# Reordering the prologue of a Fourier-mixing and gated-FFN kernel: loads, fillers and the stages of the first two batches

## The chip, the cores and the metric

The kernel runs on one core of one Trainium2 chip. The metric is the device time of one execution in microseconds. Before the change three runs took 904.98, 905.38 and 907.63 us; their median, 905.38, is the time before.

## What is computed

The reference mixes a sequence in the frequency domain and then applies a gated feed-forward network to every row:

```
X = rfft(x, axis=1);  Y = X * (filt_r + 1j*filt_i);  y = irfft(Y, n=3008, axis=1)   # x: 8 x 3008 x 256
gate = max(y @ w_gate, 0);  val = y @ w_val                                          # 256 x 1536 each
out = (gate * val) @ w_out                                                           # 1536 x 256
```

The output has 24064 rows of 256, in 32-bit floats.

## The kernel before

The 3008 points are split as 94 x 32, so that a transform is three stages of small matrix products, with two passes through DRAM ("bounces") between them.

Stage A (items_a, L269, matmul L276) is a 94-point transform: for each batch 16 items, each one 128x512 product of WA with a part of x (tiles XF, two of them, each 16 of the 32 columns wide), a copy by ScalarE into asb (L279), and after every fourth item a 384 KB write to Abuf (L281). Stage B reads Abuf back as at (load_at, L349, four loads of 384 KB), does 32-point transforms (fwd, L363), multiplies with the filters (product, L379: tt and uu; in batch 0 seven of the uu go by a ScalarE copy xs, L376, to GpSimd, L377), transforms back (inv, L393), copies (L400) and writes Dbuf (L402). There are six such excursions (i = 0 to 5) in a batch; inv of excursion i-2 stands behind fwd of excursion i. Stage C reads Dbuf back as dC (load_d, L425, four quarters of two loads), and item_c (L448) makes the transposed rows yT of one block of 512 rows. The network follows: gv (L464) makes psV and psG of one of 12 slices of the 1536 features, ScalarE copies psV (L467), VectorE multiplies (L469), and o_part (L483) makes the output of the block before.

From batch 2 on stage A is done in another way (load_chunk, fold_chunk, tiled_a; x goes through XP tiles that take the memory of the prologue). Batches 0 and 1 use items_a.

The order is written out by hand: each engine runs its instructions in the order of the program. Every DMA of SyncE goes into one queue, and a DMA that waits for a semaphore holds up those behind it; GpSimd's DMAs (filters, weights, XP) stand in order with its arithmetic. There are eight semaphores for each kind of DMA, taken in turn, so the ninth waits for the first to land.

The prologue of before: memsets of XF (L512 to L518; x has 94 rows, so some partitions stay zero), x of batch 0 by SyncE (load_x, L177) in pieces of half a tile, the DFT tables (F2, tabs, WF), and by GpSimd the filters behind a hold (hold_gpsimd, L258: a tiny copy that waits for a tile). TensorE runs 11 warm matmuls (products of a tile junk that nobody reads, L508), then the 16 items of stage A, each followed by one 128x256 filler matmul up to item 12, and by make_back_t (L193, sixteen 64x64 matmuls that transpose F2 into I2t) from item 13 on. Then come three make_back_u (L203) with six warm matmuls each, and 18 more. Meanwhile VectorE copies I2t (L198), doubles the filters in place (place_filter, L238) and places tables (L210 to L242). After the at loads SyncE issues a tiny DMA named gate (L555), which reads at and so waits until all of at is there, and only then x of batch 1. GpSimd, behind a hold on at, issues the first halves of Wv and Wg (load_vg, L246).

Then stage B of batch 0 (first_b, L405): after excursions 0 and 1 a function amid runs three fillers, after excursions 2, 3, 4 and 5 it runs 1, 2, 2 and 2 items of stage A of batch 1. Behind it stand the first quarter of dC, the tiny load "last" (L571, which waits for the last write of Dbuf), the second halves of Wv and Wg, Wo (L252), the 9 items of stage A that are left, and item_c of block 0.

The main loop (L627) runs 47 blocks of 12 steps. Work of the next batches is hung on steps (at_step): quarters 1 to 3 of dC of batch 0 on steps 0, 9 and 14, all four at loads of batch 1 on step 3, fwd of excursions 0 to 5 of batch 1 on steps 16, 23, 26, 29, 35 and 40 (end = 51), those of later batches at end - 40, -35, -28, -23, -16 and -11.

```
for i, l in enumerate((-35, -28, -25, -22, -16, -11, -4) if b == 1 else
                      (-40, -35, -28, -23, -16, -11, -4)):
```

Of the kernel before, what the change touches and what calls it, by code (L numbers as in the profile page):

```python
# [13 lines left out]
BF16 = mybir.dt.bfloat16  # L14
# [17 lines left out]
NG = 24  # L32
# [3 lines left out]
def _ap(t, offset_elems, ap_list):  # L36
    return dataclasses.replace(
        t, offset=t.offset + offset_elems, ap=[list(p) for p in ap_list]
    )
# [81 lines left out]
def kernel(  # L121
# [10 lines left out]
    nc = tc.nc  # L132
    B, S_, D = x.shape
    DFF = moe_w_gate.shape[1]
# [13 lines left out]
    dram = ctx.enter_context(tc.tile_pool(name="dram", bufs=1, space=bass.MemoryType.DRAM))  # L148
# [3 lines left out]
    pro = prologue.enter_context(tc.tile_pool(name="pro", bufs=1))  # L152

    Abuf = [dram.tile([NROW * N2, D], BF16, name=f"Abuf{b}") for b in range(B)]
    gate = dram.tile([32, 8], BF16, name="gate")
    Dbuf = [dram.tile([NROW * N2, D], BF16, name=f"Dbuf{b}") for b in range(B)]

    XF = [pro.tile([128, NX2 * D], FP32, name=f"XF{c}") for c in range(N2 // NX2)]
# [13 lines left out]
    def load_x(b, eng, cols):  # L172
        w = NX2 * D
        for c, c0, c1 in cols:
            for m in range(3):
                rows = min(32, B * N1 - (b * N1 + 32 * m))
                eng.dma_start(XF[c][m:m + 4 * rows - 3:4, c0:c1],  # L177
                              _ap(x, (b * N1 + 32 * m) * N2 * D + c * w + c0,
                                  [[N2 * D, rows], [1, c1 - c0]]))
# [7 lines left out]
    def make_back_t(q):  # L187

        psI = [ps.tile([128, 4, 64], FP32, tag=fft_tag(), name="psI") for _ in range(2)]
        for e in range(2):  # L190
            for a in range(2):
                for j in range(4):
                    nc.tensor.matmul(psI[e][64 * a:64 * a + 64, j],  # L193
                                     F2[64 * e:64 * e + 64, 12 * a + 4 * q + j, :],
                                     perm[64 * e:64 * e + 64], start=True, stop=True,
                                     tile_position=(64 * e, 64 * a))
        for e in range(2):
            nc.vector.tensor_copy(I2t[:, 8 * q + e:8 * q + 8:2, :], psI[e])  # L198
# [45 lines left out]
    def load_vg(c0, c1):  # L244
        for (w_hbm, w_sb) in ((moe_w_val, WvT), (moe_w_gate, WgT)):
            nc.gpsimd.dma_start(w_sb[:, :, c0:c1],  # L246
                                _ap(w_hbm, c0, [[DFF, 128], [128 * DFF, 2], [1, c1 - c0]]))

    def load_o():
        for c in range(2):  # L250
            nh = NFT // 2
            nc.gpsimd.dma_start(WoT[:, c * nh:(c + 1) * nh],  # L252
                                _ap(moe_w_out, c * nh * 128 * D, [[D, 128], [128 * D, nh], [1, D]]))
# [9 lines left out]
    def fft_tag(side=False):  # L263
        if side and turn.get("side"):
            return turn["side"]
        turn["i"] += 1
        return turn["tags"][turn["i"] % len(turn["tags"])]
# [76 lines left out]
    ats = {}  # L344

    def load_at(b, c):
        if c == 0:
            ats[b] = sb.tile([128, NG, D], BF16, tag="at", bufs=1, name="at")
        nc.sync.dma_start(ats[b][c:c + 125:4],  # L349
                          _ap(Abuf[b], c * NROW * NC2 * D, [[D, 32], [4 * NC2 * D, NG], [1, D]]))  # L350
# [31 lines left out]
    def inv(b, i, tags=None, cuts=CUTS):  # L382

        if i in cuts:
            dsbs[b] = i, sb.tile([128, 2, 4, D], BF16, tag="dsb", bufs=3, name="dsb")
        i0, dsb = dsbs[b]
        psD = [ps.tile([128, 2, D], FP32, tag=tags[a] if tags else fft_tag(), name="psD")
               for a in range(2)]
        for m in range(2):
            for k in range(2):  # L390
                for a in range(2):
                    for e in range(2):
                        nc.tensor.matmul(psD[a][64 * e:64 * e + 64, m],  # L393
                                         (I2t, I2u)[k][64 * a:64 * a + 64, 4 * i + 2 * m + e, :],
                                         tus[b, i, e, k][64 * a:64 * a + 64, m],
                                         start=(k == 0), stop=(k == 1),
                                         tile_position=(64 * a, 64 * e))
        o = 2 * (i - i0)
        for a in range(2):
            nc.scalar.copy(dsb[:, a, o:o + 2, :], psD[a])  # L400
        if i + 1 in cuts:
            nc.sync.dma_start(_ap(Dbuf[b], 2 * i0 * D, [[NG * D, 128], [NG // 2 * D, 2], [1, (o + 2) * D]]),  # L402
                              dsb[:, :, :o + 2, :])

    def first_b(amid):  # L405

        cuts = (0, 2, 4, 5, 6)
        for i in range(6):
            fwd(0, i)
            if i > 1:  # L410
                inv(0, i - 2, cuts=cuts)
            for e in range(2):
                product(0, i, e, 0)
                product(0, i, e, 1, pool=(i, e) in POOL_U)
            amid(i)
        inv(0, 4, cuts=cuts)
        inv(0, 5, cuts=cuts)

    dCs = {}
# [82 lines left out]
    junk = pro.tile([128, 512], BF16, tag="junk", bufs=1)  # L502

    def warm(n, cols=512):

        psJ = ps.tile([128, 512], FP32, tag=fft_tag(True), name="psJ")
        for i in range(n):
            nc.tensor.matmul(psJ[:, :cols], junk[:, 0:128], junk[:, :cols], start=True, stop=True)  # L508

    nc.sync.dma_start(WA, nc.inline_tensor(wa_h, name="dft_wa").ap())  # L510
    q = NX2 * D // 4
    nc.vector.memset(XF[0][:, 0:q], 0.0)  # L512
    nc.gpsimd.memset(XF[0][:, q:2 * q], 0.0)
    nc.vector.memset(junk, 1.0)
    nc.vector.memset(XF[0][:, 2 * q:3 * q], 0.0)
    nc.gpsimd.memset(XF[0][:, 3 * q:], 0.0)
    nc.vector.memset(XF[1][:, 0:2 * q], 0.0)
    nc.gpsimd.memset(XF[1][:, 2 * q:], 0.0)  # L518
    load_x(0, nc.sync, ((0, 0, 2 * q), (0, 2 * q, 4 * q), (1, 0, 2 * q)))
    nc.sync.dma_start(F2, nc.inline_tensor(f2_h, name="dft_f2").ap())  # L520
    nc.sync.dma_start(tabs, nc.inline_tensor(tab_h, name="dft_tab").ap())
    load_x(0, nc.sync, ((1, 2 * q, 4 * q),))
# [7 lines left out]
    warm(11)  # L530
    for i, f in enumerate(items_a(0)):
        f()
        if i >= 13:
            make_back_t(i - 13)
        else:
            warm(1, 256)
        if i == 11:
            load_at(0, 0)
    for c in range(1, 4):
        load_at(0, c)  # L540
    for half in range(2):
        for a in range(2):
            place_filter(0, a, half, nc.vector.tensor_copy)
    for i in range(3):
        make_back_u(i)
        warm(6)
    warm(18)
    place_own()
    for half in range(2):
        for a in range(2):  # L550
# [1 line left out]
    place_nyq()  # L552
    hold_gpsimd(ats[0][0:32, NG - 1, 0:8])
    load_vg(0, DFF // 2)
    nc.sync.dma_start(gate, ats[0][0:32, NG - 1, 0:8])  # L555
    load_x(1, nc.sync, ((0, 0, 2 * q), (0, 2 * q, 4 * q), (1, 0, 4 * q)))

    early = items_a(1)
# [1 line left out]
    def amid(i):  # L560
        if i < 2:
            warm(3, 256)
        else:
            for _ in range(2 if i > 2 else 1):
                next(early)()

    turn["tags"], turn["side"] = ("fft", "psv", "psg"), "pso"
    first_b(amid)
# [1 line left out]
    load_d(0, 0, 1)  # L570
    nc.gpsimd.dma_start(pro.tile([1, D], BF16, tag="last", bufs=1, name="last"),  # L571
                        _ap(Dbuf[0], (N2 * NROW - 1) * D, [[D, 1], [1, D]]))
    load_vg(DFF // 2, DFF)
    load_o()
    for f in early:
        f()
    for h in range(2):
# [13 lines left out]
    def at_step(s, f):  # L591
        side.setdefault(s, []).append(f)
# [5 lines left out]
    for b in range(1, B):  # L598
        end = (b * S // W - 1) * NFT + C_AT[0] - 5
        if b == 1:  # L600
            for c in range(4):
                at_step(3, lambda c=c: load_at(1, c))
        else:
            for j, e in enumerate((-74, -69, -64, -57)):
                l = end - 113 + NFT * j

                def next_x(b=b, j=j, l=l):
                    hold_gpsimd(yTs[l // NFT + 1][:, 0, 0:8])
                    load_chunk(b, j)
                    if j:  # L610
                        fold_chunk(b, j - 1)
                    if j == 3:
                        fold_chunk(b, j)
                at_step(l, next_x)
                at_step(end + e, lambda b=b, j=j: tiled_a(b, j))
            at_step(end + e + 4, lambda b=b: load_at_tiled(b))
        for i, l in enumerate((-35, -28, -25, -22, -16, -11, -4) if b == 1 else
                              (-40, -35, -28, -23, -16, -11, -4)):
            if i < 6:
                at_step(end + l, lambda b=b, i=i: fwd(b, i))  # L620
                for h in range(4):
                    at_step(end + l + h, lambda b=b, i=i, h=h: product(b, i, h // 2, h % 2))
            if i > 0:
                at_step(end + l, lambda b=b, i=i: inv(b, i - 1, ("psv", "psg")))
        at_step(end - 2, lambda b=b: load_d(b))
# [42 lines left out]
```

## Time and profile before

| what | us |
|---|---|
| median of three runs | 905.38 |
| the profiled execution | 907.27 |
| its span (first to last instruction) | 905.5 |
| TensorE busy in the span | 875.3 |
| stage A of batch 0, first item starts | 7.46 |
| last item of it ends (its copy starts) | 23.80 |
| stage B of batch 0, first fwd | 33.44 |
| stage B ends and the items of stage A of batch 1 that are left begin | 54.48 |
| stage C, first psY | 62.83 |
| first psV of block 0 | 63.90 |
| psY of block 1 at dC's second quarter | 75.82 |
| first fwd of batch 1 | 87.63 |

Busy us of TensorE in stretches of 10 us from 0: 6.85, 10.00, then two that the prediction shows, 7.89, 10.00, 9.11, 6.41, 8.15, 9.95; from 100 to 120 us 17.67 of 20, from 120 on 19.84 of every 20. The DMA engines' mean busy share in the first ten of these stretches is 0.64, 1.11, 1.14, 0.71, 1.00, 0.45, 1.07, 1.25, 0.97 and 0.37.

How to read it: TensorE is busy for 97% of the span, so a time is made of its work plus its gaps. A line of the waits gives who waited, for whom, the total, how often, and the longest. In the chain of waits a line is a start, a length and what ran then. A DMA's landing is the last of the sixteen increments of its semaphore.

### The profile page before, as it was taken

How to read it: one execution, taken by the hardware profiler on the slowest of the kernel's cores; microseconds unless marked ns; L12 is line 12 of the kernel's file. 1: busy time of each engine (PE TensorE's matmuls, PEld its weight loads, DVE VectorE, ACT ScalarE, POOL GpSimd, SP SyncE). 2: the span in 40 equal slices, each digit the busy share in tenths (PEclk: the TensorE clock that was granted, in tenths of full speed). 3: DMA queues.
4: the chain of work that ended last, by engine and by line, in shares of the span. 5: the costliest groups of instructions: out<-in, count | busy, mean ns of one | idle time of the engine just before them, and what ended most of it. 6: DMA issues, size and time to landing. Idle time of an engine off the chain costs nothing.

```text
span 905.5 us, 19111 instructions
## 1 busy us (share of the span) xinstructions
PE 875.3 (97%) x7096; PEld 512.1 (57%) x7217; DVE 566.6 (63%) x872; ACT 498.6 (55%) x891; POOL 359.0 (40%) x351
## 2 busy tenths in 40 slices
PE   8797899999999999999999999999999999999997
PEld 3343565556555665566655566556655556666665
DVE  2635776567665776657766677657766577655553
ACT  4474556555555555555655565655565555555552
POOL 4342667117680386614763166811768000000000
PEclk9899999999999999999999999999999999999999
DMA  9979337623475344663364533754346512331111
GB/s 254 245 219 220 101 95 177 141 80 109 122 175 118 90 126 122 141 134 112 96 161 128 119 98 101 182 116 100 108 136 158 116 31 82 78 75 36 37 32 51
DMA packets 113662, 109.17 MB, mean 121 GB/s; under 512 B 20290, under 2 KB 98370, under 8 KB 112834
## 3 DMA queue, kind: packets, MB, share of 16 engines
q1 hardware_dynamic: 91078, 81.72, 35.3%
q0 software_dynamic: 22176, 26.01, 11.7%
q8 instruction: 57, 0.93, 0.5%
q10 hardware_dynamic: 316, 0.22, 0.1%
q14 instruction: 35, 0.29, 0.1%
HBM read 61.93 MB, written 49.81 MB: 123 GB/s over the span
## 4 chain that ended last, share of the span: by engine, by line
PE 86%; DVE 4%; DMA 4%; ACT 3%; issue 1%; SPq 1%; POOL 0%; DVEq 0%; POOLq 0%
PE psG L464 25%; PE psO L483 25%; PE psV L464 24%; DVE prod L469 4%; PE psA L276 3%; PE psF L322 3%; ACT vsb L467 3%; PE psD L393 2%; PE psX L363 2%; PE psY L448 1%; DMA XF<-in_x_dram 1%; DMA dC<-Dbuf 1%; DMA Abuf<-asb 1%; DMA out_dram<-osb 0%; DMA at<-Abuf 0%
## 5 line engine op out<-in xcount | busy, mean ns | idle before, releaser
L469 DVE SCALAR_TENSOR_TENSOR prod<-psG,vsb 128x512 bf16<-128x512 f32 x564 | 389.0, 690 | 271.3 <-ACT vsb L467 265.8
L467 ACT CAST vsb<-psV 128x512 bf16<-128x512 f32 x564 | 333.0, 590 | 266.8 <-PE psV L464 211.7
L483 PE MATMUL psO<-WoT,prod 128*128 128x256 bf16 x2256 | 336.6, 273 | 1.5
L464 PE MATMUL psG<-yT,WgT 128*128 128x512 bf16 x1099 | 329.1, 379 | 7.4 <-DMA WgT<-in_moe_w_gate_dram 2.5
L464 PE MATMUL psV<-yT,WvT 128*128 128x512 bf16 x1037 | 316.9, 380 | 0.7 <-ACT yT L453 0.4
L483 PEld LDWEIGHTS <-prod 128*128 128x128 bf16 x2256 | 220.7, 98 | 143.4
L464 PEld LDWEIGHTS <-WgT 128*128 128x128 bf16 x1128 | 109.9, 98 | 136.9 <-DMA WgT<-in_moe_w_gate_dram 3.0
L464 PEld LDWEIGHTS <-WvT 128*128 128x128 bf16 x1128 | 98.1, 98 | 41.8 <-issue 30.4
L258 POOL CAST scr<-yT 128x8 f32<-128x8 bf16 x24 | 4.6, 191 | 265.8 <-ACT yT L453 265.8
L379 DVE TENSOR_TENSOR tt<-psX,Ftr 128x512 bf16<-128x512 f32 x96 | 65.0, 682 | 12.9 <-PE psX L363 12.9
L400 ACT CAST dsb<-psD 128x512 bf16<-128x512 f32 x96 | 51.5, 589 | 28.5 <-PE psD L393 28.4
L308 POOL TENSOR_TENSOR fold<-XP 128x1024 f32<-128x1024 f32 x24 | 56.5, 2356 | 25.1 <-PE psF L322 24.9
L489 ACT COPY osb<-psO 128x512 f32<-128x512 f32 x92 | 54.5, 593 | 20.6 <-PE psO L483 20.3
L379 DVE TENSOR_TENSOR uu<-psX,Fti 128x512 bf16<-128x512 f32 x89 | 60.6, 681 | 0.0
L309 POOL TENSOR_TENSOR XP<-XP 128x1024 f32<-128x1024 f32 x24 | 56.4, 2350 | 1.9
L295 POOL DMA_DIRECT2D XP<-in_x_dram x96 | 56.4, 592 | 0.9 <-issue 0.5
L453 ACT CAST yT<-psY 128x512 bf16<-128x512 f32 x47 | 27.6, 586 | 26.2 <-PE psY L448 26.2
L329 DVE CAST asb<-psF 128x512 bf16<-128x512 f32 x48 | 30.9, 686 | 17.3 <-PE psF L322 12.9
L329 ACT CAST asb<-psF 128x512 bf16<-128x512 f32 x48 | 25.8, 589 | 27.3 <-PE psF L322 27.3
L448 PE MATMUL psY<-M,dC 96*128 96x94 bf16 (+18 forms) x604 | 37.7, 198 | 1.1 <-DMA dC<-Dbuf 1.1
L455 DVE CAST yT<-psY 128x512 bf16<-128x512 f32 x47 | 32.0, 681 | 9.8 <-PE psY L448 9.8
L448 PEld LDWEIGHTS <-dC 96*128 96x128 bf16 x604 | 34.5, 97 | 4.6 <-DMA dC<-Dbuf 1.2
(66 smaller groups left out, 481.6 us busy)
## 6 DMA issues: line engine op xcount, KB each, us to landing
at<-Abuf SPq DMA_DIRECT2D x32, 384.0 KB
dC<-Dbuf SPq DMA_DIRECT2D x64, 192.0 KB
XP<-in_x_dram POOLq DMA_DIRECT2D x48, 256.0 KB, 5.9
Dbuf<-dsb SPq DMA_DIRECT2D x23, 512.0 KB
XP<-in_x_dram POOLq DMA_DIRECT2D x96, 96.0 KB, 2.7
Abuf<-asb SPq DMA_DIRECT2D x96, 96.0 KB
out_dram<-osb SPq DMA_DIRECT2D x70, 94.0 KB
XF<-in_x_dram SPq DMA_DIRECT2D x18, 256.0 KB
```

What stands on the lines that cost most here:

```text
L295: nc.gpsimd.dma_start(xp[r:r + 24, 0:4:2, :], _ap(x, (b * N1 * N2 + o) * D, [[N2 * D, 24], [47 * N2 * D, 2], [1, 512]]))
L308: tt(t, xp[:, 0:2], xp[:, 2:4], op=ALU.add)
L309: tt(xp[:, 2:4], xp[:, 0:2], xp[:, 2:4], op=ALU.subtract)
L329: copy(asf[:, :, q, :], banks[q])
L379: nc.vector.tensor_tensor(p, psX, filt, op=ALU.mult)
L400: nc.scalar.copy(dsb[:, a, o:o + 2, :], psD[a])
L448: nc.tensor.matmul(psY[:, o:o + w], dCs[b, n2 // 8][:, n2 % 8, h * 128:(h + 1) * 128], M1[:, n1:n1 + w], start=True, stop=True)
L464: nc.tensor.matmul(pt[:, :W], w[:, h, ft * 128:(ft + 1) * 128], yt[:, h, :], start=(h == 0), stop=(h == 1))
L467: nc.scalar.copy(vsb, psV[:, :W])
L469: nc.vector.scalar_tensor_tensor(prod, in0=psG[:, :W], scalar=0.0, in1=vsb, op0=ALU.max, op1=ALU.mult)
L483: nc.tensor.matmul(psO[:, t % 2], prods[ft][:, t * 128:(t + 1) * 128], WoT[:, ft, :], start=(ft == 0), stop=(ft == NFT - 1))
L489: copy(osb[:, t0 % 2:t % 2 + 1], psO[:, t0 % 2:t % 2 + 1])
```

## The change

- The first half of XF's first tile is loaded in two quarters, and the memsets ahead of it are smaller; GpSimd and VectorE each clear half of the first quarter, and junk is cleared right after.
- In stage A of batch 0 the fillers are gone. The make_back_t stand behind it, with six warm matmuls each, and the 18 warm matmuls ahead of stage B become 6.
- The gate DMA is gone: x of batch 1 is issued right behind the at loads.
- amid runs 1, 2, 2, 2 items after excursions 2 to 5, and one more between the last two inv; 8 are left behind stage B.
- The second halves of Wv and Wg are issued amid excursion 4, no longer behind "last".
- Two of the at loads of batch 1 are issued behind dC's first quarter, the two others on steps 0 and 1.
- Batch 1's stage B runs at the steps of later batches: fwd at 11, 16, 23, 28, 35 and 40.

```diff
-    gate = dram.tile([32, 8], BF16, name="gate")
...
         inv(0, 4, cuts=cuts)
+        amid(6)
         inv(0, 5, cuts=cuts)
...
-    nc.vector.memset(XF[0][:, 0:q], 0.0)
+    nc.gpsimd.memset(XF[0][:, 0:q // 2], 0.0)
+    nc.vector.memset(XF[0][:, q // 2:q], 0.0)
+    nc.vector.memset(junk, 1.0)
     nc.gpsimd.memset(XF[0][:, q:2 * q], 0.0)
-    nc.vector.memset(junk, 1.0)
...
-    load_x(0, nc.sync, ((0, 0, 2 * q), (0, 2 * q, 4 * q), (1, 0, 2 * q)))
+    load_x(0, nc.sync, ((0, 0, q), (0, q, 2 * q), (0, 2 * q, 4 * q), (1, 0, 2 * q)))
...
         f()
-        if i >= 13:
-            make_back_t(i - 13)
-        else:
-            warm(1, 256)
         if i == 11:
             load_at(0, 0)
     for c in range(1, 4):
         load_at(0, c)
+    for i in range(3):
+        make_back_t(i)
+        warm(6)
...
-    warm(18)
+    warm(6)
...
-    nc.sync.dma_start(gate, ats[0][0:32, NG - 1, 0:8])
     load_x(1, nc.sync, ((0, 0, 2 * q), (0, 2 * q, 4 * q), (1, 0, 4 * q)))
...
-            for _ in range(2 if i > 2 else 1):
+            for _ in range((1, 2, 2, 2, 1)[i - 2]):
                 next(early)()
+        if i == 4:
+            load_vg(DFF // 2, DFF)
...
-    load_vg(DFF // 2, DFF)
     load_o()
+    for c in range(2):
+        load_at(1, c)
...
-            for c in range(4):
-                at_step(3, lambda c=c: load_at(1, c))
+            for c in range(2, 4):
+                at_step(c - 2, lambda c=c: load_at(1, c))
...
-        for i, l in enumerate((-35, -28, -25, -22, -16, -11, -4) if b == 1 else
-                              (-40, -35, -28, -23, -16, -11, -4)):
+        for i, l in enumerate((-40, -35, -28, -23, -16, -11, -4)):
```

## Prediction

> **What bounds the kernel now.** I read the page first, then the waits of TensorE over the whole run and after 130 us, then the busy times by stage, the chain of waits and the timeline of VectorE, and last the landing events of every DMA (the last of the sixteen increments of its semaphore).
>
> ```profile
> PE 875.3 (97%) x7096; PEld 512.1 (57%) x7217; DVE 566.6 (63%) x872; ACT 498.6 (55%) x891; POOL 359.0 (40%) x351
> ```
>
> TensorE is the bound: only 905.5 - 875.3 = 30.2 us are not its own. The waits of TensorE say where they lie:
>
> ```profile
> PE psA L276 <- DMA XF<-in_x_dram: 4.4, 2, 3.8
> PE psG L464 <- DMA WgT<-in_moe_w_gate_dram: 2.5, 1, 2.5
> PE psJ L508 <- DVE junk L514: 2.5, 1, 2.5
> PE psX L363 <- DVE uu L379: 2.2, 2, 1.1
> PE psX L363 <- issue: 1.8, 1, 1.8
> PE psD L393 <- POOL uu L377: 1.4, 2, 0.8
> PE psY L448 <- DMA dC<-Dbuf: 1.1, 2, 0.7
> ```
>
> The same view from 130 us on has no entry at all: every stall is in the prologue and batch 1's stage B, which is what the change touches. The busy times by stage (columns: stretch, length, then busy us of PE, PEld, DVE, ACT, POOL, granted clock, DMA share, GB/s):
>
> ```profile
> 20.00:30.00 10.00, 9.95 (x83) 4.21 (x83) 6.83 (x14) 6.05 (x8) 1.00 (x2) 1.00 1.14 293
> 30.00:40.00 10.00, 5.75 (x58) 2.52 (x56) 7.13 (x12) 4.23 (x8) 5.05 (x7) 1.00 0.71 142
> 40.00:50.00 10.00, 7.89 (x57) 3.26 (x58) 3.29 (x6) 4.74 (x10) 3.37 (x3) 0.66 1.00 355
> ```
>
> The reader is to see two things: the DMA engines are full until 30 us, then have a hole, then are full again; and between 40 and 50 us TensorE's clock falls. The chain of waits names what ended last:
>
> ```profile
> 24.41 5.40 DMA Abuf<-asb
> 29.83 3.48 DMA at<-Abuf
> 33.40 0.31 SPq L555
> ...
> 34.98 6.99 DMA XF<-in_x_dram
> ...
> 65.74 9.95 DMA dC<-Dbuf
> ...
> 85.84 1.79 issue
> ```
>
> And VectorE just ahead of stage B:
>
> ```profile
> 24.07 0.76 DVE L198 CAST I2t<-psI 128x256 bf16<-128x256 f32 x2 [0.55 <-PE psI L193]
> 24.86 2.88 DVE L238 COPY Ftr<-Ftr 32x3072 bf16<-32x3072 bf16 x3
> ...
> 32.70 0.21 DVE L242 COPY Fti<-nyq 1x256 bf16<-1x256 bf16 x1
> 33.89 1.89 DVE L379 TENSOR_TENSOR tt<-psX,Ftr 128x512 bf16<-128x512 f32 x3 [0.97 <-PE psX L363]
> ```
>
> [...] the second halves of Wv and Wg (GpSimd, 59.5 and 60.2 us) took 9.96 and 12.37 us, while the 384 KB bounce write issued among them at 59.73 took 7.51 us against 2.97 for one on a quiet queue at 51.09. [...] a mean of 0.66 over 40 to 50 us is (1 - 0.66)/0.5 x 10 = 6.8 us at half clock,[...] after the 3.8 us wait at L276.
>
> **Part by part.**
> Start. The first x load waits for 512 columns of memset, not 1024: 0.91 - 0.48 us (the 0.48 from the equally wide junk memset) brings its issue from 2.02 to about 1.6. SyncE needs about 0.64 us for an x load whatever its size, and the third now carries half; third landing 7.33 before, about 5.7 after. The 11 warm matmuls end near 6.3, so stage A starts 1.1 us earlier (7.46 to 6.3).
>
> Stage A of batch 0 without filler: 13 fillers at 0.11 us (the chain) and 2 of the three make_back_t at 0.28 go: 2.0 us. But the last quarter of x landed at 18.98 and its first matmul ran at 19.12: the data were just in time. DMA is saturated (share over 1.1 from 10 to 30 us) and the change leaves the bytes ahead of that quarter as they are, so it lands at about 19.3. TensorE then waits some 2.2 us instead of running fillers, and the last 4 items of 0.86 us end at 22.9 (before 23.8). Gain 0.9.
>
> What follows it eats that. The make_back_t now stand behind: 3 x 0.28 + 3 x 0.22 + 42 warm matmuls of 0.216 = 10.6 us of TensorE, 22.9 to 33.5. VectorE's I2t copies end at about 27.2 instead of 24.8, and its fixed row of filter copies behind them (four of 0.95, three of 0.93, small ones 0.9: 7.5 us) ends at 34.7. The bounce itself is DMA-bound: Abuf's last write (landed 29.81) stands behind the same bytes; it and the last at load gain about 0.3 (33.31 to 33.0). So fwd starts at 33.5 (33.44 before), but the first product at 34.7 against 33.89: a loss of 0.8, which stays in stage B up to its first inv.
>
> Gate out. SyncE no longer waits for all of at (33.40): x of batch 1 is issued from about 30.1, behind at in the same ring, in the hole of the DMA. Its first third-set landed at 41.97; now about 35.5, ahead of its first use near 38.5. Both the 3.8 us wait and the half clock (about 4.5 us busy at half speed, 2.2) go, but next late is the xs and product work on ACT: per excursion two dsb (1.07), two asb (1.09) and an xs (0.60), 2.8 us against 2.66 measured for the undisturbed ones. Excursions 3 to 5 then end such that TensorE leaves B at about 50.0 with amid(6) (0.86) inside; before 54.55. With 8 stage-A items left, not 9, it is ready for stage C at 50.0 + 6.9 = 56.9 (before 62.4).
>
> Weights amid B. GpSimd issues them after its last uu, near 46 us, with only the "last" gate and Wo behind. They land before 56; the 2.5 us wait at ft 6 goes. The price: their bytes share the DMA with Dbuf's writes, and Abuf's second write now stands ahead of Dbuf's last. Quiet, B's end to dC landed takes 54.55 to 62.78 = 8.2 us, of which 1.7 is ACT. Add between 0 (weights done) and 4.4 us (512 descriptors of 136 ns over 16 engines, the rate at which this queue ran at 38 to 40 us); I take 2. dC lands at 50.0 + 8.2 + 2 = 60.2: TensorE waits 3.3 us there. Stage C starts 2.6 earlier, not 5.5.
>
> Next is dC's second quarter (75.68 before). In SyncE's ring it now has two at loads ahead. From the first dC's data on: 2 at loads against Wo's 1536 descriptors, 96 pairs on each engine at 74 ns (72 to 76 us before) = 7.1; two Abuf writes 2.1; its own 1.35[...]: 59.3 + 11.5 = 70.8. TensorE arrives at about 69, so psY there runs at 70.8 instead of 75.8: gain 5.0. This is the first term.
>
> The at loads of batch 1. The wait at L363 of 1.8 us (85.84) is for at, whose last part landed at 87.54. Now two parts are issued ahead and two behind dC's second quarter: last landing about 73.5; fwd at step 11 comes at about 74.5. Gain 1.8, the second term.
>
> New steps of batch 1. fwd plus inv took 0.78 us at 97.70, but 2.20 at 102.49 and 2.12 at 108.69, where fwd waited for psX buffers still read by VectorE (L379). Later batches, with the very steps (-40, -35, ...) that batch 1 gets, have no such wait. Gain 1.42 + 1.34 = 2.8, the third term.
>
> Sum: 5.0 + 1.8 + 2.8 = 9.6 us. The profiled execution took 907.27 (span 905.5), so 897.7 for it; the median of the three runs is 905.38, 1.9 lower, and the forecast for a median is 905.38 - 9.6 = **895.8**. About 0.3% (2.7 us) is what a measurement of this kernel can tell from no change.
>
> **Rivals.**
> Quiet bounce: the weights are done before Dbuf's last write. dC lands near 58, its second quarter near 68.5 and TensorE, no longer waiting, is there at 67: gain 7.3 + 4.6 = 11.9, 893.5; with a shorter stage A down to 890. For it: the DMA share of 0.45 at 50 to 60 us. Against: the bytes moved there.
> Cold stage A: without fillers the wait for x (2.2 us by my sum) grows, and the clock drops. Up to 6.8 us at half clock cost 3.4, passed on to the bounce: 9.6 - 3.4 = 6.2, 899.2; with a late dC too, 902. Against: the 2.5 us wait at L464 near 71 us did not drop the clock.
> Slower: at of batch 1. Its four loads took 12.7 to 14.0 us each, and fwd now stands 5 steps (6.5 us) earlier in TensorE's fixed order. If the last part lands as late as before (87.54), everything behind moves 6.5 later, less 2.8: +3.7, 909. It decides from a landing at 87.6 - 6.5 + 2.8 = 83.9 on. Against: half of at is issued about 10 us earlier, without weights beside it.
> No net change: the first bounce comes 3 us later and at lands at 80: 903 to 908.
>
> **How the numbers follow.** Forecast case (dC-bound, 892 to 899) 0.55; quiet bounce 0.18; cold stage A 0.14; no net change 0.06; slower 0.07. Faster: 0.55 + 0.18 + 0.14 = 0.87. The range takes the forecast case with both ends of the unknown (0 and 4.4 us at Dbuf), most of the quiet and the cold one: 890 to 902.
>
> **What would show it.** Right: a wait at L276 before item 12 of stage A; none for x near 38 us and clock 1.00 from 40 to 50; a dC wait of 2 to 5 us; none on WgT, none at L363 in batch 1. Wrong: stage A ending near 20 (x not DMA-bound), no dC wait, a wait for at at step 11.

## The result, and the profile after

The changed kernel took 909.51 us (median of four runs, 908.82 to 909.97), the kernel before 905.5 beside it (four runs): a ratio of 1.0039, 95% interval 1.0022 to 1.0057. It is slower by about 4 us, where 9.6 us less was forecast. The profiled execution of after took 909.42 us with a span of 907.6; that of before, 907.27, lies near the top of its runs (907.63 at most), so the two profiles differ by 2.1 us and the medians by 4.0. Sums below are made against the profiled executions.

After's line numbers are one below before's from L177 to L402 (L276 is now L275), and equal again at L448. The line of busy times on its page:

```profile
PE 885.3 (98%) x7210; PEld 513.3 (57%) x7210; DVE 565.6 (62%) x872; ACT 498.4 (55%) x891; POOL 359.3 (40%) x352
```

The 10.0 us of TensorE time more than before are not to be read as work. The page of before has 7096 matmuls beside 7217 weight loads, so some records are missing there, and after has 7210 of both. What that is worth shows in two kernels of the experiments below with spans of 898.2 and 898.6 us, e5 and e9: 882.2 us with 7217 matmuls and 875.7 with 7103. So the 30.2 us that the prediction called "not its own" were rather some 24, and the two totals are not compared here. Matmuls at half clock also count as busy (in after 5.78 us of the 6.8 from 42.2 to 49.0, at a granted clock of 0.50): the granted clock is read beside the waits. The waits of TensorE over the whole run (who waited for whom: total, how often, longest):

```profile
PE psY L448 <- DMA dC<-Dbuf: 5.7, 2, 5.2
PE psA L275 <- DMA XF<-in_x_dram: 5.5, 3, 2.5
...
PE psD L392 <- ACT xs L375: 1.6, 2, 1.3
PE psD L392 <- POOL uu L376: 1.1, 2, 0.7
```

The waits for Wg (2.5) and at fwd of batch 1 (1.8 and 2.2) are gone, as forecast; those for x and for dC are longer by 1.1 and 4.6. The busy times by stage, with the columns of before (PE, PEld, DVE, ACT, POOL, clock, DMA share, GB/s):

```profile
10.00:20.00 10.00, 7.29 (x16) 2.44 (x16) 0.00 (x0) 4.50 (x8) 3.46 (x7) 1.00 1.03 261
20.00:30.00 10.00, 7.93 (x51) 3.11 (x52) 1.51 (x4) 2.48 (x5) 1.09 (x3) 0.83 1.13 277
...
40.00:50.00 10.00, 7.37 (x46) 2.87 (x45) 6.04 (x10) 6.45 (x12) 6.04 (x6) 0.66 0.83 226
...
60.00:70.00 10.00, 4.84 (x12) 1.59 (x10) 0.00 (x0) 3.80 (x7) 2.17 (x3) 0.97 0.77 222
70.00:80.00 10.00, 9.67 (x41) 4.35 (x42) 4.74 (x7) 4.46 (x8) 7.04 (x4) 0.68 1.20 251
```

The clock is halved three times in the prologue (granted 0.50 from 21.7 to 25.1, 42.2 to 49.0 and 69.5 to 76.3 us); before it was once (0.50 from 40.3 to 47.1). The chain of waits of after, with the parts that answer to those shown of before:

```profile
10.85 1.50 SPq L176
12.40 1.21 SPq L176
13.65 8.18 DMA XF<-in_x_dram
22.07 5.16 PE psA L275 x8
...
36.62 0.95 DVE Fti L237
37.60 1.87 DVE Fti L237 x2
39.88 0.70 DVE tt L378
...
58.98 7.30 DMA Dbuf<-dsb
...
70.86 11.33 DMA dC<-Dbuf
```

Read from the top: the loads of x are now on the chain themselves, issue by issue. The last four items of stage A follow, then fillers and VectorE's filter copies (in before the bounce Abuf, at stood here). At the end stand the last write of Dbuf, 7.30 us where before's took 2.42, and dC's second quarter, 11.33 where it took 9.95. VectorE ahead of stage B:

```profile
30.90 0.75 DVE L197 CAST I2t<-psI 128x256 bf16<-128x256 f32 x2 [0.93 <-PE psI L192]
31.68 3.86 DVE L237 COPY Ftr<-Ftr 32x3072 bf16<-32x3072 bf16 x4
...
39.88 1.89 DVE L378 TENSOR_TENSOR tt<-psX,Ftr 128x512 bf16<-128x512 f32 x3
```

Before, VectorE was done with its copies at 32.91 and waited 0.97 us for psX, and the first product ran at 33.89; now psX is there (fwd at 38.03) and VectorE is not, because I2t, which stands ahead of its copies, comes 6.8 us later (31.65 against 24.83). The first product is 6.0 us later. The forecast had the mechanism, with a loss of 0.8.

The stages side by side, in us of the profiled executions:

| | before | forecast | after | e4 | e5 | e9 | e13 |
|---|---|---|---|---|---|---|---|
| last quarter of x lands | 18.98 | 19.3 | 21.83 | 18.94 | | | |
| stage A of batch 0 ends | 23.77 | 22.9 | 27.23 | 23.90 | 23.61 | 23.71 | 23.84 |
| first product | 33.89 | 34.7 | 39.88 | 34.42 | 33.89 | 33.55 | 33.97 |
| stage B ends | 54.55 | 50.0 | 57.80 | 52.91 | 51.04 | 50.09 | 50.50 |
| first quarter of dC lands | 62.78 | 60.2 | 69.94 | 65.46 | 60.47 | 60.41 | 61.18 |
| second quarter of dC lands | 75.68 | 70.8 | 82.19 | 77.55 | 72.66 | 73.08 | 68.98 |
| first o_part | 80.04 | | 87.11 | 82.47 | 77.58 | 78.01 | 77.34 |

Each column is one execution. How much such times scatter shows where the code is the same: with x in halves and the fillers in place (before, e4 to e6, e9 to e14) the last quarter of x landed between 17.43 and 19.35, and the first product ran between 33.55 and 34.91. Smaller differences in these two rows are not read.

### The profile page after: what moved, and what is told of

Same layout as the page of the kernel before. It is cut to its first block, busy times and chain, and to the rows that moved or that the text cites. A ratio compares the mean times of both kernels' runs of the same rounds, so it can differ in the third digit from the quotient of the medians.

```text
span 907.6 us, 19225 instructions
## 1 busy us (share of the span) xinstructions
PE 885.3 (98%) x7210; PEld 513.3 (57%) x7210; DVE 565.6 (62%) x872; ACT 498.4 (55%) x891; POOL 359.3 (40%) x352
## 3 DMA queue, kind: packets, MB, share of 16 engines
q0 software_dynamic: 22176, 26.01, 12.1%
## 4 chain that ended last, share of the span: by engine, by line
PE 92%; DMA 4%; SPq 2%; DVE 1%; ACT 1%; issue 0%; POOL 0%; DVEq 0%
PE psV L464 27%; PE psO L483 27%; PE psG L464 26%; PE psF L321 3%; PE psY L448 2%; PE psD L392 2%; PE psX L362 2%; PE psA L275 1%; DMA dC<-Dbuf 1%; SPq L176 1%; DMA XF<-in_x_dram 1%; DMA Dbuf<-dsb 1%; PE psJ L508 1%; DMA out_dram<-osb 1%; DVE Fti L237 0%
## 5 line engine op out<-in xcount | busy, mean ns | idle before, releaser
L464 PE MATMUL psV<-yT,WvT 128*128 128x512 bf16 x1128 | 337.7, 381 | 0.2 <-ACT yT L453 0.2
L464 PE MATMUL psG<-yT,WgT 128*128 128x512 bf16 x1128 | 336.6, 380 | 0.0
L448 PE MATMUL psY<-M,dC 96*128 96x94 bf16 (+18 forms) x604 | 38.1, 200 | 5.7 <-DMA dC<-Dbuf 5.7
L328 DVE CAST asb<-psF 128x512 bf16<-128x512 f32 x48 | 30.9, 686 | 17.3 <-PE psF L321 12.4
L455 DVE CAST yT<-psY 128x512 bf16<-128x512 f32 x47 | 32.0, 680 | 15.3 <-PE psY L448 15.3
L448 PEld LDWEIGHTS <-dC 96*128 96x128 bf16 x604 | 34.9, 98 | 9.1 <-DMA dC<-Dbuf 6.1
```

The costliest lines, as they stand in the source:

```text
L328: copy(asf[:, :, q, :], banks[q])
L448: nc.tensor.matmul(psY[:, o:o + w], dCs[b, n2 // 8][:, n2 % 8, h * 128:(h + 1) * 128], M1[:, n1:n1 + w], start=True, stop=True)
L464: nc.tensor.matmul(pt[:, :W], w[:, h, ft * 128:(ft + 1) * 128], yt[:, h, :], start=(h == 0), stop=(h == 1))
```

## The experiments

The theory that the first comparison suggested: the fourth load of x makes the data of stage A late, TensorE runs dry and cold, and what is lost there reaches dC; and the weights amid excursion 4 hold Dbuf's writes. Its rivals: it is the fillers that were taken out; or it is the weights alone. Unless said otherwise an edit is made to after.

### Which part makes stage A late: e1, e3, e7, e8, e4

e1 loads x in halves again, with the memsets of before:

```diff
...
-    load_x(0, nc.sync, ((0, 0, q), (0, q, 2 * q), (0, 2 * q, 4 * q), (1, 0, 2 * q)))
+    load_x(0, nc.sync, ((0, 0, 2 * q), (0, 2 * q, 4 * q), (1, 0, 2 * q)))
```

> The changed kernel with x of batch 0 loaded in halves again (and the memsets of before), all else as changed. Theory 1 (the quarters: six loads of half the size take SyncE 0.6 us each like whole ones, so the second tile of x is issued some 1.4 us later and meets the filter loads in the DMA; TensorE runs dry three times and its clock falls): the last quarter of x lands near 19 instead of 21.8, stage A ends at 22.6 instead of 27.2 at full clock, first fwd near 33.5, and the time falls by 4 to 6 us to 903.5 to 905.5. Rival 2 (what costs is the weights amid stage B that hold up Dbuf's writes): stage B only starts earlier, the wait for dC grows by as much, and the time stays within 1.5 us of 909.5.

Measured: 904.54 us, ratio to before 0.9974 (0.9965 to 0.9983): (1.0039 - 0.9974) x 905.5, about 5.9 us less than after. The last of x landed at 17.30, stage A ended at 21.43, the clock stayed full there, and the first product ran at 34.20.

e3 keeps the quarters and puts one 128x256 filler behind each item of stage A:

```diff
         f()
+        warm(1, 256)
```

> The changed kernel with one 128x256 filler matmul behind every item of stage A again; the make_back_t stay behind it and x stays in quarters. It tells the clock from the data: Theory 1 with the data alone: x lands as late, the waits for x stay near 5.5 us less the 1.8 us of fillers, and stage A ends near 26 to 27; with the clock alone: the clock stays full and stage A ends 1.5 us earlier. Time 907.5 to 909.5 either way, since the fillers fill no gap of 2.5 us.

Measured: 910.22 us, 1.0042 (1.0028 to 1.0055), as after. The clock was halved all the same, at 23.2 us: one filler of 0.11 us between two items doesn't fill waits of 1.4 to 2.5. Stage A ended at 28.29.

e7 is before with nothing but the quarters and the memsets of after:

```diff
...
-    load_x(0, nc.sync, ((0, 0, 2 * q), (0, 2 * q, 4 * q), (1, 0, 2 * q)))
+    load_x(0, nc.sync, ((0, 0, q), (0, q, 2 * q), (0, 2 * q, 4 * q), (1, 0, 2 * q)))
```

> The kernel before with nothing but x's first half in quarters and the memsets that go with it. Theory 1: its last quarter of x lands near 21.8 instead of 19.0, stage A ends 2.5 to 3 us later and the bounce behind it too; what follows waits for x of batch 1 behind the gate as before: 2 to 4 us slower. The rival (only together with the missing fillers does it cost): within 1 us of before.

Measured: 908.29 us, 1.0013 (0.9995 to 1.0030), not to be told from no change; the 2 to 4 us that the theory asked for did not come. Stage A ended 2.4 us later (26.16) and the first product ran 2.0 later (35.85), but the clock kept full there and the first o_part came 1.2 later. So the quarters alone delay the first product by 2.0 us, and in after by 5.7 (39.88 against 34.20 in e1), where make_back_t, the warm matmuls and VectorE's copies stand behind stage A's end. The 5.9 us of e1 are thus the price of the quarters together with the rest of the change, and not of the quarters by themselves.

e8 asks why the last quarter is late. It holds back the filters, GpSimd's first DMAs, until XF's second tile is there:

```diff
-    hold_gpsimd(XF[0][:, 2 * q - 8:2 * q])
+    hold_gpsimd(XF[1][:, 2 * q - 8:2 * q])
```

> The changed kernel with the filters held until the third quarter of x (first half of XF's second tile) has landed, not the second eighth. It tells what delays x: if the filters' packets in the same DMA engines do, the last quarter of x lands near 18 to 19, stage A ends at 22 to 23 at full clock, and the time falls by 3 to 5 us; the filters end some 1 us later and may take one us back at the filter copies. If SyncE's issue times alone do (six loads of 0.6 us), the last quarter lands near 21 and the time stays within 1.5 us of 909.5.

Measured: 907.09 us, 0.9991 (0.9975 to 1.0008), about 4.3 us less than after. The last of x landed at 17.86 and stage A ended at 21.85, with the quarters in. So the bytes beside it, the filters', are what the later loads run into. But the filters then landed at 32.1, the last of at at 36.76 (33.31 before) and fwd at 37.01: what was taken from x was handed to the bounce.

All the traces together bear this out: in the four executions with quarters and the filters beside them (after, e2, e3, e7) the last of x landed between 21.26 and 22.51, in the eleven with halves between 17.30 and 19.35, and in e8 at 17.86.

e4 is e1 with the stage A of before as well (fillers, make_back_t within, 18 warm matmuls behind):

```diff
         f()
+        if i >= 13:
+            make_back_t(i - 13)
+        else:
+            warm(1, 256)
...
-    for i in range(3):
-        make_back_t(i)
-        warm(6)
...
-    warm(6)
+    warm(18)
```

> The changed kernel with all of the old start: x in halves, fillers, make_back_t amid the last items, 18 warm matmuls ahead of stage B; the rest (no gate, items and weights amid B, at loads, steps of batch 1) as changed. Theory 1: stage A ends at 23.8, first fwd at 33.4, no wait for x near 38, stage B ends near 50 to 51, dC near 62, no waits for WgT and at: 899 to 901. Rival 2: as e1, dC still 12 us behind B's end and TensorE cold after it: 904 to 907.

Measured: 903.63 us, 0.9971 (0.9961 to 0.9980), within 0.9 us of e1, and short of the 899 to 901 that the theory asked for: dC's first quarter landed at 65.46 and not near 62. Taking the fillers out brings stage A's end 2.5 us forward in e1 and fwd 0.2. So the rival "fillers" falls as an explanation of its own, and so does what was hoped from their removal: fwd waits for the bounce.

### The weights amid stage B: e2, e5

e2 puts the second halves of Wv and Wg back behind the load "last":

```diff
-        if i == 4:
-            load_vg(DFF // 2, DFF)
...
+    load_vg(DFF // 2, DFF)
     load_o()
```

> The changed kernel with the second halves of Wv and Wg behind the last write of Dbuf again, all else as changed. Theory 1: stage A is untouched; dC's first quarter lands near 66.4 instead of 69.9, but the 2.5 us wait for WgT comes back and dC's second quarter stays near 82: time within 2 us of 909.5. Rival 2: the whole of dC's 7 us lateness goes, psY near 63, and the time falls by 4 us or more, below 905.5.

Measured: 911.83 us, 1.0060 (1.0045 to 1.0075), no gain. Its chain of waits (start, length, what):

```profile
58.92 3.11 DMA Dbuf<-dsb
...
62.43 3.43 DMA dC<-Dbuf
...
69.33 13.07 DMA dC<-Dbuf
```

The mechanism is confirmed: without the weights Dbuf's last write takes 3.11 us, not 7.30, and dC's first quarter lands at 65.86, 4.1 earlier. But its second quarter lands at 82.40, where it did (82.19): the weights' bytes are now ahead of that one. The wait is moved, not removed: TensorE now waits 5.63 us for the second one. The wait for Wg that was expected back did not come; Wg landed at 72.09 and its second half was first used at 74.48.

e5 is e4 with the weights issued two excursions earlier, far from Dbuf's last write:

```diff
-        if i == 4:
+        if i == 2:
             load_vg(DFF // 2, DFF)
```

> The kernel of e4 (old start, the rest as changed) with the second halves of Wv and Wg issued after excursion 2 instead of 4. If the weights are what holds up the writes of Dbuf (in e4 dC landed 12.5 us after stage B's last matmul, 8.2 before the change), they now pass ahead of those writes: dC lands 9 us or less after B's end, near 62 instead of 65.5, TensorE waits 2 to 3 us there instead of 5.6 and keeps its clock; the time falls by 1 to 3 us below e4. If instead the later chain (Wo, at, dC's second quarter) sets the pace, dC's second quarter lands no earlier than 1 us before e4's and the time stays within 1 us of e4.

Measured: 900.84 us, 0.9922 (0.9895 to 0.9948), faster than both kernels, and than before by some 6 to 7 us; than e4 by 2.8 (medians) to 4.4 (ratios). Dbuf's last write took 4.36 us, dC's quarters landed 5 us earlier than in e4, at 60.47 and 72.66, and the first o_part was at 77.58.

### The steps of batch 1 and the gate, each alone: e6, e12

e6 is before with only the new steps of batch 1 (fwd at 11, 16, 23, 28, 35 and 40):

```diff
-        for i, l in enumerate((-35, -28, -25, -22, -16, -11, -4) if b == 1 else
-                              (-40, -35, -28, -23, -16, -11, -4)):
+        for i, l in enumerate((-40, -35, -28, -23, -16, -11, -4)):
```

> The kernel before with nothing but the new steps of batch 1 (fwd at 11, 16, 23, 28, 35 and 40; the at loads stay on step 3). By the third term of the prediction the two waits of fwd for psX buffers go: 2.8 us less. The rival: fwd stands five steps earlier while at still lands near 87.5, so TensorE waits 6 us longer at step 11 and the whole is 3 to 4 us slower.

Measured: 912.65 us, 1.0060 (1.0041 to 1.0080). One line of its waits says why:

```profile
PE psX L363 <- DMA at<-Abuf: 9.9, 2, 8.9
```

at landed at 86.89, about as in before (87.54), and fwd stood in front of it. This is the "slower" rival of the forecast, at its place: it put that case at +3.7 and it costs 5.7. Its sum had no clock in it, which here stood at half from 80.8 to 91.0; how much of the difference that makes was not tried. The steps are a gain only with at issued earlier; in after at's last load landed at 85.53 and fwd ran at 85.62, just in time because the steps ahead of it were late as well.

e12 is before without the gate DMA and its tile, nothing else:

```diff
-    gate = dram.tile([32, 8], BF16, name="gate")
...
-    nc.sync.dma_start(gate, ats[0][0:32, NG - 1, 0:8])
```

> The kernel before with the gate DMA taken out, nothing else. By the prediction the 3.8 us wait for x and 2.2 us of half clock go and stage B ends 5 us earlier, with the rest given back at dC's second quarter, which lands 2 to 4 us earlier: 2 to 4 us faster. By what e4 showed (clock halved all the same, GpSimd's uu late): stage B ends only 2 to 2.5 us earlier and the time falls by 1 to 2 us.

Measured: 903.27 us, 0.9968 (0.9956 to 0.9981): 3 us, about all that e4 has. TensorE left stage B at 51.87 instead of 54.55, without a wait for x of batch 1. The profiled execution, 908.28, is one of the slowest of its 22 runs (900.84 to 908.46), so its stages are no more than an example; its clock fell again at 69.8 and 86.9.

### What is left ahead of the second quarter: e9, e10, e11, e13, e14

Even e5 has the second quarter at 72.7, and from 60 us on, where its 2.4 us wait for dC's first one ends, the clock is halved for some 3.4 us (a mean of 0.83 from 60 to 70).

e9 adds to e5 eight fillers ahead of the first inv of batch 0, where TensorE waits for xs and uu:

```diff
+                if i == 2:
+                    warm(8)
```

> The kernel of e5 with eight warm matmuls (1.7 us) ahead of the first inv of stage B, where TensorE waits for GpSimd's uu anyway. It prices the half clock in stage B: if the low activity there (and not only the old wait for x) drops the clock, it now stays full from 33 to 58 us and stage B ends 1 to 2 us earlier, near 49.5. If the next link is the DMA (dC, then dC's second quarter), that gain is given back at dC and the time stays within 1 us of e5; else it falls by 1 to 2 us.

Measured: 900.66 us, 0.9938 (0.9926 to 0.9950). The clock stays full through stage B (1.00 from 30 to 50), which ends 0.95 us earlier than e5's, but dC's quarters land no earlier (60.41, 73.08). The 0.95 us, of which 0.34 came from an earlier first product, is given back there. Its stages:

```profile
40.00:50.00 10.00, 9.91 (x108) 4.19 (x107) 5.64 (x10) 9.24 (x19) 5.62 (x6) 1.00 1.09 280
60.00:70.00 10.00, 8.88 (x42) 4.02 (x44) 5.07 (x8) 4.69 (x8) 7.04 (x4) 0.83 1.18 240
```

TensorE is full from 40 to 50 now, and the DMA share is over 1 in both stretches.

e10 is e5 with all four at loads of batch 1 on step 0, behind dC's second quarter in the queue:

```diff
-    for c in range(2):
-        load_at(1, c)
...
-            for c in range(2, 4):
-                at_step(c - 2, lambda c=c: load_at(1, c))
+            for c in range(4):
+                at_step(0, lambda c=c: load_at(1, c))
```

> The kernel of e5 with all at loads of batch 1 behind dC's second quarter in SyncE's queue. If the two at loads ahead of it are what holds dC's second quarter (11 us from issue to landing in e4 and e5), it lands near 67 instead of 72.7, the 1.4 us wait for it at psY goes, and at lands near 74.5 and costs 1 us at step 11: 1 to 2 us faster than e5. If Wo on GpSimd's queue holds it, it lands no earlier than 71 and the time stays within 1 us.

Measured: 903.22 us, 0.9965 (0.9951 to 0.9979), slower than e5 by 2.4. The quarter lands at 70.46, only 2.2 us earlier, and the price, with a clock halved behind it from 76.5 to 83.4, is higher:

```profile
PE psX L362 <- DMA at<-Abuf: 4.2, 2, 3.6
```

e11 puts e9, e10 and ten warm matmuls ahead of item_c of block 0 together; against e10:

```diff
+                if i == 2:
+                    warm(8)
...
+    warm(10)
```

> e9 and e10 together, with ten warm matmuls ahead of stage C so that the clock lives through the wait for dC. If clock and DMA order are the two things that the sum of the prediction left out, clock 1.00 throughout from 10 us on and 897 to 899.5; if one of them only moves the wait, 900 to 901.

Measured: 904.04 us, 0.9978 (0.9970 to 0.9986): nothing over e10 and above both expectations, though the clock was halved only once in its whole prologue, at 79.3.

What had stayed beside the quarter in e10 was Wo. e13 is e9 with Wo held until the second quarter has landed:

```diff
-    load_o()
...
+    at_step(0, lambda: (hold_gpsimd(dCs[0, 1][:, 0, 0:8]), load_o()))
```

> The kernel of e9 with Wo issued on step 0 behind a hold on dC's second quarter, no longer right behind the load named last. If Wo's bytes are what holds dC's second quarter (72 to 73 us in e5 and e9, 70.5 with nothing but Wo beside it in e10): it lands near 67, the at loads at 69 to 75, TensorE has no wait for it, Wo lands at 72 to 77, and the time is 2 to 3 us below e9's 900.7. The rival, that the quarter is late by its own place in the queue and its own writes: it still lands at 70 or later and the time is within 1 us of e9's. The risk is that Wo comes after the first o_part wants it (about 75 us): then a wait there takes back what was gained.

Measured: 901.20 us, 0.9949 (0.9937 to 0.9962). The quarter lands at 68.98, 4.1 us earlier than in e9, so Wo's bytes were what held it; the expected gain of 2 to 3 us didn't come. Its waits show where it went:

```profile
PE psY L450 <- DMA dC<-Dbuf: 3.7, 1, 3.7
...
PE psO L485 <- DMA WoT<-in_moe_w_out_dram: 1.0, 2, 0.7
PE psX L362 <- DMA at<-Abuf: 0.9, 1, 0.9
```

The wait for the second quarter, 1.83 us in e9 and so all that could be won at it, is gone; Wo itself lands at 79.27 and is waited for, and the first o_part comes only 0.7 us earlier (77.34).

e14 adds ten warm matmuls to e13, ahead of item_c of block 0:

```diff
+    warm(10)
```

> e13 with ten warm matmuls ahead of item_c of block 0, so that TensorE's clock is kept through the wait for dC's first quarter. If a halved clock behind that wait still costs time once nothing else is late there: 1 us less than e13. If TensorE waits for data again behind it, the same as e13 within 0.5 us.

Measured: 901.31 us, 0.9948 (0.9934 to 0.9961), as e13. In the profiled execution the clock kept full behind dC's first quarter, but it fell at 36.0 in stage B instead, where it was full in e13, and stage B ended 2.1 us later (52.55). So the times show no price of the halved clock behind dC's first quarter; that it has none is not shown.

The intervals of e5, e9 and e13 overlap; none of the three can be called the best. Each is faster than both kernels, by about 4 to 7 us against before.

## Why the prediction was wrong

It named TensorE's gaps in the prologue rightly, and its second and third terms (1.8 and 2.8) hold in their sum; no run parts them. From psY at dC's second quarter to the end before took 907.27 - 75.82 = 831.45 us and after 909.42 - 82.33 = 827.09, a gain of 4.4 against 4.6. The first term failed: that psY ran at 82.33, not at 70.8. Before and after:

```profile
75.82 0.28 PE L448 MATMUL psY<-M,dC 96*128 96x94 bf16 x3 [0.74 <-DMA dC<-Dbuf]
...
82.33 0.28 PE L448 MATMUL psY<-M,dC 96*128 96x94 bf16 x3 [0.45 <-DMA dC<-Dbuf]
```

These 11.5 us are nearly the whole miss of the sum (897.7 for the profiled execution, 909.42 measured). They divide, by the forecast's own steps, into:

| from, to | forecast | measured | miss |
|---|---|---|---|
| start to first product | 34.7 | 39.88 | 5.2 |
| first product to the end of B | 15.3 | 17.92 | 2.6 |
| end of B to dC landed | 10.2 | 12.1 | 1.9 |
| dC's first to psY at its second quarter | 10.6 | 12.4 | 1.8 |

**The failing step** is in stage A: "the change leaves the bytes ahead of that quarter as they are, so it lands at about 19.3". It landed at 21.83. The bytes ahead were counted and the issues were not, although the step before had the number: "SyncE needs about 0.64 us for an x load whatever its size". SyncE's queue of before (start, length, engine and line, what, how many):

```profile
4.58 3.14 SPq L177 DMA_DIRECT2D XF<-in_x_dram  x5
...
8.92 1.88 SPq L177 DMA_DIRECT2D XF<-in_x_dram  x3
```

and of after:

```profile
4.68 4.42 SPq L176 DMA_DIRECT2D XF<-in_x_dram  x7
9.15 0.70 SPq L521 DMA_DIRECT2D F<-dft_f  x1
9.89 0.87 SPq L522 DMA_DIRECT2D tabs<-dft_tab  x1
10.85 3.39 SPq L176 DMA_DIRECT2D XF<-in_x_dram  x3
```

Splitting three loads in two makes three issues more, and the issue of the last quarter's loads begins at 10.85 instead of 8.92. The filters, whose issue on GpSimd begins at 8.03 in before and at 7.97 in after, did not move, and so went ahead of them. x lost its lead over the filters' bytes. The last of the three loads was out at 14.24 instead of 10.80. Of these 3.4 us the three issues more are 1.9 (7.61 us for twelve loads, 5.69 for nine) and longer issues behind them 2.0 (3.39 against 1.88 for the last three, 1.70 against 1.16 from F to there), less the 0.5 by which the first one started earlier. One issue is small beside its load (a median of 0.59 us, for 128 KB as for 256 KB, and 2.5 to 8.8 us from issue to landing); what counted here is the sum of the issues in one queue. e1 (17.30 without the quarters), e7 (21.26 with nothing but the quarters) and e8 (17.86 without the filters beside it) show this. TensorE in stage A of after:

```profile
5.67 3.66 PE L275 MATMUL psA<-XF,WA 128*96 128x512 f32 x8
10.81 3.64 PE L275 MATMUL psA<-XF,WA 128*96 128x512 f32 x8 [1.48 <-DMA XF<-in_x_dram]
15.89 3.65 PE L275 MATMUL psA<-XF,WA 128*96 128x512 f32 x8 [1.43 <-DMA XF<-in_x_dram]
22.07 5.16 PE L275 MATMUL psA<-XF,WA 128*96 128x512 f32 x8 [2.54 <-DMA XF<-in_x_dram]
```

The second, third and fourth group of four items wait, and the last takes 5.16 us instead of 3.65, at half clock. Of the 4.3 us by which stage A ends late, 2.5 are the landing and 1.5 the half clock (5.16 - 3.65), the "cold stage A" rival. That rival was priced at 3.4 at most for the clock; what it lacked was a later landing. The rest of the first row: the row from stage A's end to fwd took 10.8 us (forecast 10.6) and the filter copies 8.2 up to the first product (7.5). Mending this step alone (e1) brings 5.9 of the 13.7 us between forecast and result; the rest lies in the steps below.

**B itself.** "Clock 1.00 from 40 to 50" failed, with x of batch 1 in time (its first three loads landed by 39.15, later than the 35.5 of the forecast; first use 44.4). The clock fell at other waits: TensorE waited for xs and uu, 1.25, 0.30, 0.34 and 0.75 us between 40 and 43.6. The late first product is not what it takes: in e4 and e5, with the first product at 34.42 and 33.89, waits of 0.30, 0.55 and 0.84 us stand in the same place, and the clock fell as well (37.7 and 38.2). That the clock can fall behind waits as short as these was not in the working. e9, which fills that place, has the clock full (1.00 from 40 to 50) and B from first product to end in 16.5 us, still 1.2 over the forecast's 15.3.

**Weights.** The 2 us taken for them at Dbuf lie inside the ends that were given (0 to 4.4): 3.9 in after, by 12.1 against a quiet 8.2. Mechanism right, size low. What the weights' bytes do to a write issued among them shows in Dbuf's last one: 3.11 us without them beside it (e2), 7.30 with them.

**dC's second quarter.** From dC's first landing, 12.2 us in e5 and 9.8 in e10, which is e5 with at moved behind it; 12.7 in e9 and 7.8 in e13, which is e9 with Wo moved behind it. So at is worth about 2.4 and Wo about 5, and the forecast's 10.6 had at and Wo as its main parts and was short by 1.8 of 12.4. Before's trace has about as many packets of each queue while both move, 874 of SyncE's and 848 of GpSimd's from 72 to 76 us, 74 ns for a pair on 16 engines, as the forecast had it. The 11.5 us also hold 0.9 from the last data to the landing, the author's estimate, which is not shown: for dC's first quarter before's trace has 0.49 (last packet done at 62.29, landing at 62.78). But in after TensorE waits only 0.45 us for this quarter: behind the late first one it ran at half clock (69.5 to 76.3) and was itself not there before 81.9, where the forecast had it waiting from 69 on.

**Rivals.** The rival "slower" named 909, which is the number measured, by chance: its mechanism, TensorE standing at fwd of batch 1 for at, is not in after (at's last load landed at 85.53 and fwd ran at 85.62, with no wait for at). Nearest in mechanism is the rival "no net change", a first bounce 3 us late: at of batch 0 landed 2.8 us later (36.15 against 33.31). It was given 0.06, and the time lies 1.5 us above its range.

**Where the expected gain went.** Even with stage A mended and the weights moved (e5), the 9.6 us came to 6 or 7. In e13 the bytes were put in the order in which TensorE wants them, and the wait only went from one load to the next. Over the first 78 us the mean busy share of the DMA engines is 0.91 in before and 0.97 in e9 and 0.98 in e13. The forecast read the holes of that share (0.71 and 0.45) as room, which they were, but a small one: (0.98 - 0.91) x 78 = 5.5 us of DMA time in all, of which TensorE's first o_part got 2.0 to 2.7. That the DMA engines' total now sets this start is a reading of these shares; single stretches go above 1 (up to 1.25), so it is no exact limit, and cutting bytes was not tried.

Not settled: why the 8.2 us from B's end to dC became 9.4 to 10.7 in e5, e9 and e13 with the weights landed by 53.3 in e5; Abuf's second write, whose share was not tried alone, is one thing ahead of it.

## What to carry to other kernels

Count issues as well as bytes: a load split in two took SyncE's queue twice as long here (0.59 us for each issue, at 128 KB as at 256), and the issue of the loads behind began 1.9 us later (10.85 against 8.92) while the other queue's did not move. Where DMA is nearly full (a mean share of 0.97 and 0.98 over the first 78 us in e9 and e13), an earlier start of one transfer was paid by another (e2, e8, e13), so name the next load to be late before counting a gain, and look at the sum of the DMA shares over the whole stage first. Steps that are made for data that comes earlier must be tried together with what brings the data; alone they can cost more than they give.

## What was not expected of the hardware

The length of a wait does not tell by itself whether the clock falls. In after it fell at 21.7, 42.2 and 69.5 us, and in before at 40.3; in the prologue the stretches at a granted clock of 0.50 lasted 3.41 us (the one at 21.7) or 6.83 (the other three). The third wait for x in stage A of after took 2.54 us, from 19.53 to 22.07, and the clock fell 2.2 us into it. The wait for Wg in before took 2.54 us too (70.10 to 72.64), and the clock stayed at 1.00. In e12 the same wait took 2.94 us (up to 70.17), and the clock fell 2.6 us into it, at 69.8. The prediction had taken the wait in before as evidence against a cold stage A; with a wait of the same length the clock fell in after, so it was none. What kept the clock in before is not shown.

Nor is a single long wait at every fall. The fall of after at 69.5 came 4.7 us into the 5.24 us wait for dC, but the waits around the one at 42.2 were of 1.25, 0.30 and 0.34 us, between 40 and 42.5. The fall of before, which the prediction put behind the 3.8 us wait for x, came within it, 2.0 us from its start (38.31 to 42.11, the fall at 40.3). These runs do not tell how much idle time is enough.

SyncE took 1.50 and 1.21 us to issue two of the 256 KB loads of x, at 10.85 and 12.40 us in after, against a median of 0.59 us for these loads. The filters were going out on GpSimd's queue then. But so they were in before, where the same loads took at most 0.59 us; with the filters held back (e8) the longest took 0.73. What makes an issue slow is open.
